# One attention kernel with filling: the maxima of q, k and v and their scales' chains queued behind a tick's row maxima, and the casts and a batch's last splitting spread over more slots

## The chip, the cores and the metric

The kernel runs on one core of a Trainium2 chip. What counts is the device time of one execution in microseconds (us), as a median over several runs. Engines are named as the profile names them: PE is TensorE's matrix multiplication and PEld its loading of weights, DVE is VectorE, ACT is ScalarE, POOL is GpSimd, SP is SyncE, which here issues most of the transfers.

## The reference, cut to what matters

Three stages are chained: block-causal attention, a layer of eight experts with a router, and a gated MLP. Inputs are float32. q and k are drawn with a spread of 0.1 and multiplied by about 3.98.

```python
def _attn_ref(q, k, v):                    # B, H, S, D = 4, 8, 576, 64
    scores = D ** -0.5 * np.matmul(q, k.transpose(0, 1, 3, 2))
    mask = block_i >= block_j              # blocks of 64 positions
    scores = np.where(mask, scores, -1e9)
    attn = np.exp(scores - scores.max(-1))
    attn = attn / (attn.sum(-1) + 1e-9)
    return np.matmul(attn, v)

def _moe_ref(x, w_gate, w1, w2):           # N, D, E, F = 2304, 512, 8, 1024
    P = np.exp(x @ w_gate - (x @ w_gate).max())
    for _ in range(8):
        P /= P.sum(1) + 1e-9
        P /= P.sum(0) + 1e-9
        P *= N / E
    return sum(P[:, e] * (np.maximum(x @ w1[e], 0) @ w2[e]) for e in range(E))

def _moe2_ref(x, w_gate, w_val, w_out):    # 512 -> 1536 -> 512
    g = x @ w_gate
    return (g / (1 + np.exp(-g)) * (x @ w_val)) @ w_out
```

## The kernel before, in words

**The whole.** Matrix products run in float16 with every operand split into a high part and a low part (the cast of a scaled value, and what the cast left out), and 2x2 blocks of matrices are multiplied with seven products instead of eight, over sums and differences of the blocks. So for each operand there is work on ScalarE (the cast, "hi") and on VectorE or POOL (the rest, "lo"). The attention's output goes into `xs`, the seven split operands of the next stage, without a trip to memory. The kernel's rough course is attention with filling to about 350 us, then the experts, then the gated MLP.

**The attention.** `attention` goes over 16 pairs of heads, four to a batch element ("batch" below). A pair takes eight ticks `u` (`TICKS`, L822): u = 0 and 1 hold two score blocks each, u = 2 to 5 one, u = 6 and 7 the two halves of the last. The ticks of the next pair follow without a break, and each tick does a step of several ticks: scores of tick tk (`scores`, L986), their row maxima on VectorE (`maxima`, L999), exponentials of tk - 1 on ScalarE (`exps`, L1016), the reciprocals of the row sums on VectorE (`normalise`, L1031 to L1036) and the scaling on POOL (L1041) of tk - 2, and the transposes on TensorE (L1064, L1073) with the copies on ScalarE (L1067, L1074) of tk - 4. `values` (L1091) multiplies with v at u = 6 and, for the pair before, at u = 4. A tick has three sub-steps, which end in a `yield` each. In each engine the instructions stand in the order in which this code issues them, and an instruction that waits holds up those behind it on its engine. Scores take one of three banks of PSUM (`ps_s`), which a tick frees with its exponentials.

**What lies beside a pair.** From the second batch on, q and k of a pair are split too. `load_qk` loads them, `max_qk` (L917 to L920) takes the maximum of each on VectorE, `across_mid` (L110) brings the maxima of all partitions together with one matmul, `scale_qk` (L116, L156 to L164, L926 to L931) makes the scale from it by a chain of small VectorE operations, `hi_qk` (L937) casts on ScalarE, and `lo_qk` (L941) takes the rest on VectorE and issues the copies into `st` on SP's queue. v needs one scale for a batch: `scan_load`, `scan_max` (L883), `scale_v_begin` (L889), `across_mid`, `scale_v_end` (L895 to L901). `at(tick, f)` (L1164) enters these in a table, and a tick runs its entries first of all, ahead of its scores.

**The output's splitting.** `take` (L1100) writes the attention's output to `xf` (L1106, ScalarE) and puts three or six pieces of splitting work into the queue `pend`: sums on POOL (L1133), casts on ScalarE or POOL (L189, L191), rests on VectorE or POOL (L194, L1124). `work(n)` (L1158) does the first n of them: one or two in a tick, all that is left at u = 4, and at the end of a batch (u = 4 of the next pair) the six new ones at once, after which `ready` says how many rows of the next stage may be worked on.

**Filling.** `first_part` is work of the next stage that runs between the attention's ticks: for the first three of five blocks of 256 rows (`NEARLY` = 3) the router's logits (L1255, L1263) and two expert units (u = 0, 1) with `expert_in` and `plain_out`. While `ready` isn't zero, 47 of 96 sub-steps pull one step of it; what is left after the attention runs by itself. A step of `products_in` (L548) is six matmuls. Sums of products are made on ScalarE (L575) and VectorE (L572, L579, L581, L587), and `plain` turns each of the four sums of a unit into the split operand `m_h`: a cast with Relu on ScalarE (L775) and the rest on VectorE (L779). `later(d, f)` (L510) puts f d slots behind, where a slot is a step of products, that is a call of `tick`. `bank` hands out three banks for these products in turn (their names begin with abc), and `row_bank` gives the small products of `across_mid` one of these as long as `ready` is zero, and one of the scores' banks after that. Through the first half of the attention the weights of both units are split too (`w0`, lines L377, L179, L183).

Names in the profile leave out numbers: `m_h` is the operand of an expert unit, `m_t` and `abc_m_c` a sum and a bank of it, `s` scores, `e` exponentials, `a` the transposed ones, `t` the bank of the transposes, `x` that of the values, `hl` the split q and k, `qk_r`, `qk_e`, `qk_i`, `qk_s` the steps of their scale.

Of the kernel before, what the change touches and what calls it, by code (L numbers as in the profile page):

```python
# [30 lines left out]
def attention_moe_glu_kernel(  # L31
# [724 lines left out]
    def expert_in(u, b, bank):  # L756

        h = hts[u, b] = {}
        if b == BOTH:
            parts = [(units[v][0], *blocks[NB - 1], v == u) for v in (u, u + 1)]  # L760
        else:
            parts = [(units[u][0], *blocks[b], b == NB - 1 or (u % 2 == 1 and u > 1 and b == NB - 2))]
        n = sum(p[2] for p in parts)
        name = f"m{u}_{b}"
        q = {}

        def plain(t, half, src, spare):
            h[t, half] = places.take(f"{name}_h{t}{half}")
            hi, lo = h[t, half][:, 0, :, :n], h[t, half][:, 1, :, :n]
            s = src[:, :, :n]  # L770
            if spare is not None:
                places.give(spare)

            def first():
                nc.scalar.activation(hi, s, AF.Relu)  # L775
                later(1, rest)

            def rest():
                nc.vector.scalar_tensor_tensor(lo, s, 0.0, hi, op0=ALU.max, op1=ALU.subtract)  # L779
                if (t, half) != (1, 0) or b >= NEARLY:  # L780
                    places.give(src)

            if (t, half) == (1, 1):
                later(3 if n == TB else 1, first)
            elif (t, half) == (1, 0) and b >= NEARLY:
                r = places.take(f"{name}_r", F32)
                nc.scalar.copy(r[:, :, :n], s)
                src, s = r, r[:, :, :n]
                later(2, first)
            else:  # L790
                first()

        def quad(t, half, src, spare):
            q[t, half] = src
            if spare is not None:
                q["spare"] = spare
            if (t, half) == (1, 0):
                r = places.take(f"{name}_r", F32)
                nc.scalar.activation(r[:, :, :n], src[:, :, :n], AF.Relu)
                sums_out(h, name, n, q[0, 0], q[0, 1], r, q[1, 1], q["spare"], True)  # L800
                return
            o = {(0, 0): X11, (0, 1): X12, (1, 1): X22}[t, half]
            later(3 if o == X22 and n == TB else 2, lambda: later(1, operand(h, o, name, n, src, AF.Relu)))

        yield from products_in(name, parts, bank, plain if u < 2 else quad)
# [25 lines left out]
    def attention(actx):  # L831
# [19 lines left out]
        zero = const.tile([P, 1], F32, name="zero")  # L851
        nc.gpsimd.memset(zero, 0.0)
        pend = deque()
        for c in range(NC):
            w = ((c + 1) * CB + P - 1) // P * P
            et[c] = ap.tile([P, w], F32, tag=f"e{c}", name=f"e{c}")
            if w > (c + 1) * CB:
                nc.gpsimd.memset(et[c][:, (c + 1) * CB :], 0.0)
# [299 lines left out]
        def work(n):  # L1158
            for _ in range(min(n, len(pend))):
                pend.popleft()()  # L1160

        events = {}

        def at(tick, f, *a):  # L1164
            events.setdefault(tick, []).append(lambda: f(*a))

        for p in range(1, npairs):
            r = p * NTK
            if p < DIRECT:
                if p > 1:  # L1170
                    at(r - NTK, load_direct, p)
                    at(r - 2, lambda p: vt.update({p: load_v(*where(p), "v", 2)}), p)
                continue
            for i in range(2):
                if p > 1:
                    at(r - 14 + 1 * i, load_qk, p, i)
                at(r - 11 + i, max_qk, p, i)
                at(r - 6 + 2 * i, hi_qk, p, i)
                at(r - 5 + 1 * i, lo_qk, p, i)
            at(r - 8, lambda p: across_mid(st[p]["m"]), p)  # L1180
            at(r - 7, scale_qk, p)
            at(r - 2, lambda p: vt.update({p: load_v(*where(p), "v", 2)}), p)
        for b in range(B):
            r = (b - 1) * NPAIR * NTK
            for i in range(NPAIR):
                if b:
                    at(r + i * NTK + (0 if i else 3), scan_load, b, i)
                at(r + i * NTK + NTK if b else 1 + i, scan_max, b, i if b else ORDER[i])
            r = r + NPAIR * NTK if b else NPAIR
            at(r, scale_v_begin, b)  # L1190
            at(r + (2 if b else 1), lambda b: across_mid(vmx[b]), b)
            at(r + (3 if b else 2), scale_v_end, b)

# [12 lines left out]
        for tk in range(tot + NTK):  # L1206
# [7 lines left out]
                scores(p, u)  # L1214
            if u == 6 and p < npairs:
                take(p, 0, values(p, 0))
            yield
            out1 = None
            if on(tk - 4):
                out1 = transposes(*divmod(tk - 4, NTK))  # L1220
            work(2 if len(pend) > 6 else 1)
            if on(tk - 2):
                normalise(*divmod(tk - 2, NTK))
            if out1:
                out1()
            if on(tk):
                maxima(p, u)
            yield

            if p and u == 4:  # L1230
# [1 line left out]
                take(p - 1, 1, values(p - 1, 1))  # L1232
                st.pop(p - 1)
                vt.pop(p - 1)
                if p % NPAIR == 0:
                    work(len(pend))
                    ready[0] = p // NPAIR * S // 2
            if p and u == 3:
                rest(p - 1)()
            if on(tk - 1):  # L1240
                exps(*divmod(tk - 1, NTK))
            yield


# [619 lines left out]
```

## Time and profile before

| what | value |
| --- | --- |
| median of three runs | 2028.02 us (2029.44, 2022.48, 2028.02) |
| the profiled execution | 2023.14 us, its span 2021.4 us |
| TensorE's mean granted clock | 0.99 |
| busy share: PE, DVE, ACT, POOL | 96%, 79%, 68%, 31% |

The span is the time from the first to the last instruction that the profiler recorded in one execution; the profiled execution's own time is 1.7 us longer. "Granted clock" is the share of its full clock (2.4 GHz) that TensorE was given: 0.50 is the lower of its two levels, 1.2 GHz. A mean of 0.99 means that little of the span ran at the lower one. A busy share is an average over stages that are limited by different things, so the rows below come from stretches of the attention and not from the whole.

### The profile page before, as it was taken

Reading aid. Unit: us, or ns where it says so; the run is one execution under the profiler, and the core shown is the slowest. Engines: PE = TensorE matmul, PEld = TensorE weight load, DVE = VectorE, ACT = ScalarE, POOL = GpSimd, SP = SyncE. Lnnn points to the kernel's source line nnn. Section 1 sums busy time; section 2 is a strip of 40 time slices with the busy share of each in tenths; the row PEclk is TensorE's granted clock in tenths of the full one; section 3 lists DMA queues with packets and bytes.
Section 4 is the critical chain, followed back from the end, with each engine's and each line's share of the span. In section 5 each row is a group of like instructions: output and inputs, shape, how many; then the busy total and the mean of one; then the engine's idle time right before and its main releaser. Section 6 shows DMA issues by size and latency. Waiting matters only on the chain. (4 is left out here: it accounts for less than half of the span.)

```text
span 2021.4 us, 47060 instructions
## 1 busy us (share of the span) xinstructions
PE 1939.9 (96%) x18378; PEld 1670.5 (83%) x18378; DVE 1594.6 (79%) x3404; ACT 1382.3 (68%) x2880; POOL 620.5 (31%) x876
## 2 busy tenths in 40 slices
PE   7789999999999999999999999999999889999998
PEld 3457767889888988978888898898889778888987
DVE  8886774888889788798978889778886887667666
ACT  6766775477777788777877877778776656544442
POOL 5544443013333333333333333333332232000000
PEclk9899999999999999999999999999999999999999
DMA  5333432226777786777768768677776100301112
GB/s 154 110 104 112 121 87 63 104 59 136 153 176 158 148 170 129 170 157 160 172 132 167 159 135 178 131 164 162 144 175 152 38 12 17 95 1 53 33 43 53
DMA packets 168079, 236.72 MB, mean 117 GB/s; under 512 B 16432, under 2 KB 84656, under 8 KB 167856
## 3 DMA queue, kind: packets, MB, share of 16 engines
q0 software_dynamic: 67136, 108.29, 31.0%
q1 hardware_dynamic: 100720, 125.42, 19.9%
q8 instruction: 144, 2.36, 0.5%
q14 instruction: 79, 0.65, 0.1%
HBM read 90.39 MB, written 24.38 MB: 57 GB/s over the span
## 5 line engine op out<-in xcount | busy, mean ns | idle before, releaser
L548 PEld LDWEIGHTS <-w 128*128 128x128 f16 x6720 | 609.5, 98 | 79.6 <-issue 16.3
L658 PEld LDWEIGHTS <-m_h 128*128 128x128 f16 x5292 | 513.4, 98 | 69.9 <-issue 6.7
L1519 POOL DMA_DIRECT2D acc<-ev x354 | 311.9, 927 | 576.4 <-ACT ev L1523 377.9
L548 PE MATMUL abc_m_b<-xs,w 128*128 128x256 f16 (+1 forms) x3840 | 474.1, 263 | 7.1 <-ACT m_t L575 3.7
L658 PE MATMUL m_o_b<-w,m_h 128*128 128x256 f16 x3024 | 404.1, 273 | 9.8 <-ACT ev L1523 6.0
L658 PE MATMUL m_o_ac<-w,m_h 128*128 128x256 f16 x2268 | 309.4, 273 | 0.0
L548 PE MATMUL abc_m_c<-xs,w 128*128 128x256 f16 (+1 forms) x1920 | 227.8, 263 | 0.0
L1523 ACT ACTIVATE ev<-m_o_b,pe 128x256 f32<-128x256 f32 x354 | 163.9, 480 | 66.7 <-PE m_o_b L658 45.4
L1523 ACT ACTIVATE ev<-m_o_ac,pe 128x256 f32<-128x256 f32 x236 | 136.3, 580 | 44.5 <-PE m_o_ac L658 43.1
L183 DVE SCALAR_TENSOR_TENSOR w<-wr,ws,w 128x512 f16<-128x512 f32 x210 | 155.6, 750 | 8.3 <-ACT w L179 8.3
L179 ACT ACTIVATE w<-wr,ws 128x512 f16<-128x512 f32 x210 | 150.1, 724 | 17.1 <-DVE ws L164 12.3
L194 DVE TENSOR_TENSOR m_h<-m_t,m_h 128x512 f16<-128x512 f32 x189 | 129.4, 686 | 32.4 <-ACT m_h L696 31.5
L696 ACT CAST m_h<-m_t 128x512 f16<-128x512 f32 x189 | 117.2, 620 | 28.0 <-DVE m_t L720 26.7
L689 ACT ACTIVATE m_h<-m_t 128x512 f16<-128x512 f32 x189 | 118.3, 626 | 23.8 <-DVE m_t L587 14.9
L548 PEld LDWEIGHTS <-gg_w 128*128 128x128 f16 x1260 | 114.6, 98 | 22.0 <-issue 10.0
L693 DVE SCALAR_TENSOR_TENSOR m_h<-m_t,m_h 128x512 f16<-128x512 f32 x189 | 128.5, 684 | 3.1 <-ACT m_h L689 2.8
L1506 POOL DMA_DIRECT2D acc<-ev_s x52 | 63.1, 1213 | 217.0 <-ACT ev_s L1499 211.7
L548 PEld LDWEIGHTS <-gv_w 128*128 128x128 f16 x1260 | 114.5, 98 | 14.0 <-issue 2.2
L658 PEld LDWEIGHTS <-g_h 128*128 128x128 f16 x1134 | 111.5, 99 | 16.3 <-issue 2.3
L1041 POOL TENSOR_SCALAR e<-e,r 128x64 f32<-128x64 f32 (+2 forms) x144 | 84.4, 592 | 124.9 <-DVE r L1036 72.1
L548 PE MATMUL abc_m_a<-xs,w 128*128 128x256 f16 (+1 forms) x960 | 117.5, 262 | 0.0
L572 DVE TENSOR_TENSOR m_t<-m_t,abc_m_b 128x512 f32<-128x512 f32 x73 | 49.4, 677 | 68.2 <-PE abc_m_b L548 60.1
(320 smaller groups left out, 3390.7 us busy)
## 6 DMA issues: line engine op xcount, KB each, us to landing
acc<-ev POOLq DMA_DIRECT2D x354, 256.0 KB, 4.3
wr<-in_w_dram SPq DMA_DIRECT2D x128, 256.0 KB, 5.2
acc<-ev_s POOLq DMA_DIRECT2D x52, 256.0 KB, 3.9
st<-hl SPq DMA_DIRECT2D x48, 144.0 KB, 3.5
raw_g<-in_w_gate_dram SPq DMA_DIRECT2D x12, 512.0 KB, 4.7
raw_v<-in_w_val_dram SPq DMA_DIRECT2D x12, 512.0 KB, 5.2
raw_o<-in_w_out_dram SPq DMA_DIRECT2D x12, 512.0 KB, 5.0
scr_g<-gg SPq DMA_DIRECT2D x21, 256.0 KB, 3.2
```

The source lines that it names most:

```text
L179: nc.scalar.activation(hi, src, AF.Copy, scale=s)
L183: nc.vector.scalar_tensor_tensor(lo, src, s, hi, op0=ALU.mult, op1=ALU.subtract)
L194: nc.vector.tensor_sub(lo, src, hi)
L548: nc.tensor.matmul(ps[:, f, to : to + w], W[o][:, sh, k, f * P : (f + 1) * P], xs[:, o, mh, k, c0 : c0 + w], start=x not in begun, stop=Tr ...
L658: nc.tensor.matmul(ps, h[o][:, sh, k, ii * P : (ii + 1) * P], W[o][:, mh, k], start=o in (X11, X12) and k == 0 and j == 0, stop=True, skip ...
L689: nc.scalar.activation(hi, src, AF.Relu)
L693: nc.vector.scalar_tensor_tensor(lo, src, 0.0, hi, op0=ALU.max, op1=ALU.subtract)
L696: nc.scalar.copy(hi, src)
L1041: nc.gpsimd.tensor_scalar(et[c][:, :n], et[c][:, :n], g["r"][:, c : c + 1], 1.0, op0=ALU.mult, op1=ALU.mult)
L1506: nc.gpsimd.dma_start(acc[:, x - 1 : x + 1, cols], e, accum_op=ALU.add)
L1519: nc.gpsimd.dma_start(acc[:, x], e, accum_op=ALU.add)
L1523: nc.scalar.activation(e[:, cols], ps, AF.Copy, scale=p)
```

## The change

It has three parts. No instruction is added or removed; instructions move in their engines' queues.

1. In `plain`, the rest (L779) of the three early blocks comes two slots behind its cast instead of one, and the cast of a whole block's first two sums joins the queue one slot later instead of at once.
2. At the end of a batch, the six pieces of splitting are no longer done at once: `hurry` counts them, and `hurried()` does one per sub-step, in the other places of a tick too. `ready` is raised when the last is done, six sub-steps later. The last batch still does them at once.
3. `max_qk`, `scale_qk`, `scan_max` and `scale_v_begin` are entered in a second table (`after`, `behind_maxima`), which a tick runs behind its row maxima, at the end of its second sub-step, instead of ahead of its scores. `across_mid`, `scale_v_end`, `hi_qk` and `lo_qk` stay where they were.

```diff
--- before.py
+++ after.py
@@ -773,7 +773,7 @@
 
             def first():
                 nc.scalar.activation(hi, s, AF.Relu)
-                later(1, rest)
+                later(1 if b >= NEARLY else 2, rest)
 
             def rest():
                 nc.vector.scalar_tensor_tensor(lo, s, 0.0, hi, op0=ALU.max, op1=ALU.subtract)
@@ -787,6 +787,8 @@
                 nc.scalar.copy(r[:, :, :n], s)
                 src, s = r, r[:, :, :n]
                 later(2, first)
+            elif n == TB:
+                later(1, first)
             else:
                 first()
 
@@ -851,6 +853,7 @@
         zero = const.tile([P, 1], F32, name="zero")
         nc.gpsimd.memset(zero, 0.0)
         pend = deque()
+        hurry = [0]
         for c in range(NC):
             w = ((c + 1) * CB + P - 1) // P * P
             et[c] = ap.tile([P, w], F32, tag=f"e{c}", name=f"e{c}")
@@ -1159,10 +1162,22 @@
             for _ in range(min(n, len(pend))):
                 pend.popleft()()
 
+        def hurried():
+            if hurry[0]:
+                work(1)
+                hurry[0] -= 1
+                if not hurry[0]:
+                    ready[0] += S // 2
+
         events = {}
 
         def at(tick, f, *a):
             events.setdefault(tick, []).append(lambda: f(*a))
+
+        behind_maxima = {}
+
+        def after(tick, f, *a):
+            behind_maxima.setdefault(tick, []).append(lambda: f(*a))
 
         for p in range(1, npairs):
             r = p * NTK
@@ -1174,20 +1189,20 @@
             for i in range(2):
                 if p > 1:
                     at(r - 14 + 1 * i, load_qk, p, i)
-                at(r - 11 + i, max_qk, p, i)
+                after(r - 11 + i, max_qk, p, i)
                 at(r - 6 + 2 * i, hi_qk, p, i)
                 at(r - 5 + 1 * i, lo_qk, p, i)
             at(r - 8, lambda p: across_mid(st[p]["m"]), p)
-            at(r - 7, scale_qk, p)
+            after(r - 7, scale_qk, p)
             at(r - 2, lambda p: vt.update({p: load_v(*where(p), "v", 2)}), p)
         for b in range(B):
             r = (b - 1) * NPAIR * NTK
             for i in range(NPAIR):
                 if b:
                     at(r + i * NTK + (0 if i else 3), scan_load, b, i)
-                at(r + i * NTK + NTK if b else 1 + i, scan_max, b, i if b else ORDER[i])
+                after(r + i * NTK + NTK if b else 1 + i, scan_max, b, i if b else ORDER[i])
             r = r + NPAIR * NTK if b else NPAIR
-            at(r, scale_v_begin, b)
+            after(r, scale_v_begin, b)
             at(r + (2 if b else 1), lambda b: across_mid(vmx[b]), b)
             at(r + (3 if b else 2), scale_v_end, b)
 
@@ -1214,17 +1229,23 @@
                 scores(p, u)
             if u == 6 and p < npairs:
                 take(p, 0, values(p, 0))
+            hurried()
             yield
             out1 = None
             if on(tk - 4):
                 out1 = transposes(*divmod(tk - 4, NTK))
-            work(2 if len(pend) > 6 else 1)
+            if hurry[0]:
+                hurried()
+            else:
+                work(2 if len(pend) > 6 else 1)
             if on(tk - 2):
                 normalise(*divmod(tk - 2, NTK))
             if out1:
                 out1()
             if on(tk):
                 maxima(p, u)
+            for f in behind_maxima.pop(tk, ()):
+                f()
             yield
 
             if p and u == 4:
@@ -1232,13 +1253,17 @@
                 take(p - 1, 1, values(p - 1, 1))
                 st.pop(p - 1)
                 vt.pop(p - 1)
-                if p % NPAIR == 0:
+                if p == npairs:
                     work(len(pend))
-                    ready[0] = p // NPAIR * S // 2
+                    ready[0] = B * S // 2
+                elif p % NPAIR == 0:
+                    hurry[0] = len(pend)
             if p and u == 3:
                 rest(p - 1)()
             if on(tk - 1):
                 exps(*divmod(tk - 1, NTK))
+            if u != 4:
+                hurried()
             yield
 
 
```

What moves is seen in the order of the instructions on an engine. The first place is VectorE at the start of pair 7, while block 0's first unit is worked on. In the rows, `vmx` is the maximum of v, `bias` that of the rows, and `qk_r` to `sc` the chain of the next pair's q and k. Before:

```order
L779 SCALAR_TENSOR_TENSOR m_0_h_1882<-m_0_t_1880,m_0_h_1882 128x512
L883 TENSOR_REDUCE vmx_1286<-vs_2_1619 128x1
L999 ISA junk,bias_1971<-qk_a,zero,sc_1671 128x64
L999 ISA bias_1971 128x1
L999 ISA junk,bias_1971<-qk_a,zero,sc_1671 128x128
L999 ISA bias_1971 128x1
L779 SCALAR_TENSOR_TENSOR m_0_h_1998<-abc_m_0_b,m_0_h_1998 128x512
L116 TENSOR_REDUCE qk_r<-qk_a 128x2
L156 TENSOR_SCALAR qk_e<-qk_r 128x2
L163 TENSOR_SCALAR qk_i<-qk_e 128x2
L164 RECIPROCAL qk_s<-qk_i 128x2
L931 TENSOR_SCALAR sc_2011<-qk_i 128x1 x2
```

With the change (the lines are three further down in the file):

```order
L779 SCALAR_TENSOR_TENSOR m_0_h_1882<-m_0_t_1880,m_0_h_1882 128x512
L1002 ISA junk,bias_1946<-qk_a,zero,sc_1676 128x64
L1002 ISA bias_1946 128x1
L1002 ISA junk,bias_1946<-qk_a,zero,sc_1676 128x128
L1002 ISA bias_1946 128x1
L886 TENSOR_REDUCE vmx_1294<-vs_2_1594 128x1
L587 TENSOR_TENSOR m_0_t_1823<-m_0_t_1823,abc_m_0_c 128x512
L1034 TENSOR_SCALAR r_1600<-sum_1599 128x1
L1039 RECIPROCAL r_1600<-r_1600 128x1
L1002 ISA junk,bias_1946<-s_1_1976,zero,sc_1676 128x192
L1002 ISA bias_1946 128x1
L1002 ISA junk,bias_1946<-s_1_1976,zero,sc_1676 128x256
```

The maximum of v now stands behind the first row maxima, and the chain of q and k has left these rows: it follows the row maxima of u = 1, whose last is the row 128x256.

The second place is ScalarE at the end of pair 6 and the start of pair 7, with two casts of `plain` to `m_h` and the copies of the transposed exponentials to `a`. Before:

```order
L1016 ACTIVATE e_140,sum_1624<-s_5_1844,bias_1623,sc_1338 128x512
L775 ACTIVATE m_0_h_1942<-m_0_t_1742 128x512
L775 ACTIVATE m_0_h_1882<-m_0_t_1880 128x512
L1074 COPY a_6_1904<-t_3_1946 128x3x128
L1074 COPY a_6_1904<-t_4_1982 128x4x128
L775 ACTIVATE m_0_h_1998<-abc_m_0_b 128x512
L1016 ACTIVATE e_141,sum_1624<-s_6_1891,bias_1623,sc_1338 128x288
L1016 ACTIVATE e_141,sum_1624<-s_7_1930,bias_1623,sc_1338 128x288
L1074 COPY a_6_1904<-t_5_2036 128x4x128
```

With the change:

```order
L1019 ACTIVATE e_140,sum_1599<-s_5_1825,bias_1598,sc_1341 128x512
L1077 COPY a_6_1884<-t_3_1919 128x3x128
L1077 COPY a_6_1884<-t_4_1957 128x4x128
L1019 ACTIVATE e_141,sum_1599<-s_6_1861,bias_1598,sc_1341 128x288
L1019 ACTIVATE e_141,sum_1599<-s_7_1908,bias_1598,sc_1341 128x288
L775 ACTIVATE m_0_h_1938<-m_0_t_1936 128x512
L775 ACTIVATE m_0_h_1992<-m_0_t_1823 128x512
L1077 COPY a_6_1884<-t_5_1995 128x4x128
```

The two casts have moved from ahead of two copies and two exponentials to behind them; the next copy still follows them.

The third place is ScalarE at the end of the first batch, u = 4 to 6 of pair 4. `xs` are the casts of the batch's last splitting, `w` is weights' splitting. Before:

```order
L1106 ACTIVATE xf_3_1_1120<-x_1_1109,vs_263 128x320
L191 CAST xs<-xf_3_1_1120 128x160 x2
L191 CAST xs<-xf_2_1_863 128x160
L1016 ACTIVATE e_137,sum_948<-s_3_1064,bias_947,sc_742 128x384
L1067 COPY a_4_1099<-t_1_1152 128x2x256
L179 ACTIVATE w_1_0_1162<-wr_0_00_884,ws_0_1138 128x512
L1263 COPY lsb_1197<-abc_lg_1164 128x64
L1016 ACTIVATE e_138,sum_948<-s_4_1094,bias_947,sc_742 128x448
```

With the change:

```order
L1109 ACTIVATE xf_3_1_1120<-x_1_1109,vs_263 128x320
L1019 ACTIVATE e_137,sum_943<-s_3_1064,bias_942,sc_759 128x384
L191 CAST xs<-xf_3_1_1120 128x160 x2
L1070 COPY a_4_1099<-t_1_1139 128x2x256
L179 ACTIVATE w_1_0_1154<-wr_0_00_884,ws_0_1125 128x512
L1019 ACTIVATE e_138,sum_943<-s_4_1094,bias_942,sc_759 128x448
L191 CAST xs<-xf_2_1_863 128x160
```

The three casts no longer stand together ahead of the exponential of u = 3, and the logits' copy `lsb` has left these rows, since filling starts later.

## Rows read from the trace of the kernel before

**Rows 1.** Busy time by window: us, busy (instructions), PEclk, DMA share, GB/s.

```profile
58.00:92.00 34.00, 27.50 (x201) 15.30 (x202) 29.13 (x104) 22.95 (x62) 21.51 (x46) 0.80 0.52 145
92.00:142.00 50.00, 39.54 (x355) 27.35 (x354) 45.34 (x140) 37.16 (x94) 20.68 (x41) 0.98 0.36 105
169.00:346.00 177.00, 171.94 (x1618) 125.89 (x1617) 121.53 (x444) 121.84 (x328) 81.35 (x185) 1.00 0.31 88
```

The busy columns are PE, PEld, DVE, ACT and POOL, in this order.

**Rows 2.** The same view, the windows of lower clock.

```profile
75.20:82.00 6.80, 6.07 (x23) 2.96 (x25) 6.10 (x25) 3.65 (x10) 4.57 (x14) 0.50 0.31 84
85.40:88.80 3.40, 3.40 (x48) 2.52 (x46) 2.65 (x13) 1.72 (x4) 2.24 (x6) 0.50 0.84 218
140.04:146.87 6.83, 5.33 (x29) 3.64 (x30) 5.94 (x22) 3.69 (x9) 2.12 (x5) 0.50 0.16 47
```

**Rows 3.** Timeline: start, duration, engine, line, [idle before, its releaser].

```profile
139.11 0.67 DVE L587 TENSOR_TENSOR m_t<-m_t,abc_m_c 128x512 f32<-128x512 f32 x1
139.88 1.15 ACT L775 ACTIVATE m_h<-m_t 128x512 f16<-128x512 f32 x2 [2.88 <-DVE m_t L587]
...
141.54 1.09 PE L1073 MATMUL t<-ident,e 128*128 128x128 f32 x4 [3.54 <-ACT a L1074]
```

**Rows 4.** Timeline, TensorE: waits behind ScalarE at four other places.

```profile
104.62 0.41 PE L1064 MATMUL t<-ident,e 128*128 128x128 f32 x2 [1.26 <-ACT a L1074]
...
113.81 0.44 PE L986 MATMUL s<-st,st 128*64 128x288 f16 x4 [1.26 <-ACT xf L1106]
...
228.44 0.63 PE L1073 MATMUL t<-ident,e 128*128 128x128 f32 x4 [0.80 <-ACT a L1074]
...
312.73 0.63 PE L1073 MATMUL t<-ident,e 128*128 128x128 f32 x4 [1.14 <-ACT a L1074]
```

**Rows 5.** Timeline, the end of the first batch's splitting.

```profile
84.12 0.33 ACT L191 CAST xs<-xf 128x160 f16<-128x160 f32 x1 [0.23 <-POOL xf L1133]
...
85.16 0.84 PE L986 MATMUL s<-st,st 128*64 128x512 f16 x4 [2.01 <-ACT e L1016]
```

**Rows 6.** Timeline, three pairs' starts, and a step of filling.

```profile
75.60 1.11 PE L1073 MATMUL t<-ident,e 128*128 128x128 f32 x4 [2.32 <-POOL e L1041]
...
76.02 0.55 ACT L1016 ACTIVATE e<-s,bias,sc 128x256 f32<-128x256 f32 x1
...
76.86 0.96 PE L986 MATMUL s<-st,st 128*64 128x448 f16 x4
...
90.31 0.82 PE L548 MATMUL abc_m_b<-xs,w 128*128 128x256 f16 x6
...
100.68 0.66 PE L1073 MATMUL t<-ident,e 128*128 128x128 f32 x4 [1.31 <-POOL e L1041]
...
120.28 0.41 DVE L116 TENSOR_REDUCE qk_r<-qk_a 128x2 f32<-128x256 f32 x1
...
121.14 0.17 DVE L164 RECIPROCAL qk_s<-qk_i 128x2 f32<-128x2 f32 x1
...
121.56 0.77 ACT L937 ACTIVATE hl<-qk,qk_s 128x576 f16<-128x576 f32 x1
...
124.05 0.51 ACT L1016 ACTIVATE e<-s,bias,sc 128x192 f32<-128x192 f32 x1 [1.72 <-DVE bias L999]
...
124.14 0.66 PE L1073 MATMUL t<-ident,e 128*128 128x128 f32 x4 [1.90 <-POOL e L1041]
```

**Rows 7.** Timeline, two splittings of VectorE and POOL's scaling.

```profile
140.54 0.69 DVE L779 SCALAR_TENSOR_TENSOR m_h<-m_t,m_h 128x512 f16<-128x512 f32 x1 [0.76 <-ACT m_h L775]
...
141.90 0.69 POOL L1041 TENSOR_SCALAR e<-e,r 128x512 f32<-128x512 f32 x1 [2.52 <-DVE r L1036]
...
142.13 1.00 DVE L779 SCALAR_TENSOR_TENSOR m_h<-m_t,m_h 128x512 f16<-128x512 f32 x1
```

**Rows 8.** Timeline, TensorE at the end of the attention.

```profile
346.11 2.27 PE L1091 MATMUL x<-a,v 128*64 128x320 f32 x20 [0.73 <-ACT a L1074]
...
349.01 0.55 PE L1255 MATMUL m_lg<-wg,xs 128*128 128x16 f16 x15 [0.62 <-ACT xf L1106]
```

## The prediction

> **What bounds the kernel now.** I read the page's busy shares first, then the views in this order: busy time by stretch, the stretches at half clock, the timeline at each of TensorE's longer waits, and the order of instructions of both kernels. Over the whole span TensorE is busy 96%, so time can be gained only where it idles or runs at half clock. The instruction orders of both kernels are the same from the third block's logits on, but for two casts and their splittings in one block; whatever happens, happens in the first 370 us. [Rows 1] split the attention by stretch. From 169 to 346 us TensorE is busy 171.9 of 177 us: filling has closed its gaps, and a shorter wait elsewhere gives nothing. From 58 to 142 us it is different: TensorE idles 6.5 of 34 and 10.5 of 50 us, while VectorE is busy 29.1 of 34 and 45.3 of 50. There a tick's chain (scores, row maxima on VectorE, exponentials on ScalarE, reciprocals on VectorE, scaling on POOL, transposes on TensorE, copies on ScalarE) runs beside the weights' splitting for both experts, and VectorE and the queue orders set the pace. [Rows 2] are the three stretches in which the granted clock fell to 0.50, each around a place where TensorE had waited; at half clock a stretch costs half its length where TensorE has work, so 3.4, 1.7 and 3.4 us.
>
> **The casts of filling.** In [rows 3] ScalarE stands 2.88 us before two casts to m_h, because they wait for VectorE's add L587, which had to queue (it starts at 139.11). Behind the casts stands the copy a<-t, and TensorE's next transposes wait 3.54 us for it; the clock then stays at 0.50 until 146.87 [rows 2]. The same chain (cast waits for an add, a copy or an xf behind it, TensorE behind that) is at 104.62, 113.81, 228.44 and 312.73 us [rows 4]: 1.26, 1.26, 0.80 and 1.14 us. The change lets the cast join ScalarE's queue a slot later and its splitting two slots later; no instruction is added. In the new order the casts of this place stand behind two copies and two exponentials. At 141.54 the upper bound is 3.54 + 3.4 = 6.9 us. I take 4.5, because the second cast still needs L587, which now stands behind the row maxima, vmx and a splitting, so part of the wait stays, with the next copy behind it. Of 0.80 + 1.14 = 1.9 us in the later batches I take 1.5. The two of 1.26 go into the sum for 58 to 142 us below.
>
> **The batch's last splitting.** At 84.12 ScalarE does the third of three xs casts ahead of the exponential of tick u=3, after waiting for POOL; TensorE's scores of u=5 wait 2.01 us for that exponential [rows 5], and 85.4 to 88.8 us run at half clock. In the new order the exponential comes first. Six pieces of POOL, ScalarE and VectorE work are the same in number. The broadcast w_a also goes to another bank, since `ready` is still zero, so the scores of u=5 no longer need the bank of u=3. Upper bound: 2.0 + 1.7 = 3.7 us here; at the two later batch ends only waits under half a microsecond stand.
>
> What this costs: filling starts six sub-steps (two ticks) later in each batch. It has 292 sub-steps instead of 298, at 47 steps in 96, that is 142 steps where three blocks need 135 and some waiting, so it still ends inside the attention. But about three steps leave the stretch that VectorE paces, where they were hidden, for the one that TensorE paces: 3 x 0.82 us (six matmuls of L548) [rows 6] = 2.5 us at most, 0 at least. I take 1.5. At the far end the same three steps then stand between the last values and the logits, where TensorE waits 0.73 and 0.62 us today [rows 8]: I take a gain of 1.0 of 1.35.
>
> **The maxima and chains.** The q and k chain takes VectorE from 120.28 to 121.31 [rows 6], 1.03 us, and two small operations follow. It stands ahead of the reciprocals of the pair before, whose scaling on POOL TensorE's transposes wait for: 1.90 us at 124.14, and in the same place 2.32 at 75.60 and 1.31 at 100.68 [rows 6]. Queued behind the row maxima, the chain no longer delays them: at most 3 x 1.03 = 3.1 us. But at 124.14 two m_h splittings now stand in the old place of the chain (2 x 0.69 us), so that one keeps its wait.
>
> The new wait: the hi cast of q (L937) precedes the exponentials of u=1 in ScalarE's queue in both orders. Before, the cast started at 121.56 and the exponential waited for its bias until 124.05 [rows 6]. Now the bias is ready 1.03 us sooner, but the cast waits for a chain that starts only then: 1.03 + 0.77 us after the bias, so the exponential comes 0.77 us later than before. Behind it are the scores of u=4, which need that bank. The bound from below is 0 (in the TensorE-paced batches there are some 5 us between u=1 and u=4), from above 0.77 for each of 12 pairs, 9.2 us. I take about three pairs of the VectorE-paced stretch, 2.0 us.
>
> A splitting that meets POOL runs longer: at 142.13 it takes 1.00 us beside POOL's scaling at 141.90, against 0.69 at 140.54 [rows 7]. Of block 0's eight splittings, all would cost 8 x 0.31 = 2.5 us of VectorE if each newly met one; they meet some today, so I put nothing in the sum and keep this for the range. The Trainium skill (GPSIMD Engine Reference, Key points) says that POOL shares its SBUF interfaces with VectorE and contends with VectorE instructions of two SBUF inputs; the trace agrees with the 1.00 against 0.69.
>
> **The sum.** From 58 to 142 us the separate waits that can go are 1.26 + 1.26 + 2.01 + 1.7 + about 2.1 (75.60 and 100.68) = 8.3 us. VectorE does the same work, and idles 4.9 + 4.7 = 9.5 us there [rows 1], part of it in the tiny gaps between dependent instructions; so I take about half, 4.5. Then: -4.5 (58 to 142) - 4.5 (141.54 and its clock) - 1.5 (later batches) - 1.0 (tail) + 2.0 (hi cast) + 1.5 (filling's steps) = **-8.0 us**. The profiled execution took 2023.14 us (span 2021.4), 4.9 below the median of the three runs, 2028.02; the forecast is 2015.1 on its scale, and 2020.0 on the median's.
>
> **Rivals.**
> A: VectorE is the bound from 58 to 142 us, and the waits only change places. For it: the shares of [rows 1]; no VectorE work is removed, and splittings move into the places that the chains leave. Against: VectorE itself idles in places that the change touches, as behind the burst. Then the 4.5 there is 0, a new wait of the casts keeps half of the 4.5 at 141.54, and -2.2 - 1.5 - 1.0 + 2.0 + 1.5 leaves about -1 to -2: 2026. The Trainium skill (Perfetto Trace Analysis, Identifying the Most-Contended Engine) says to optimise the engine with the highest occupancy first; by that rule this stretch would give nothing, and the trace agrees that VectorE's is the highest there (45.34 of 50 us against TensorE's 39.54).
> B: slower. The hi cast makes ScalarE late in every pair: 12 x 0.77 = 9.2 us, filling's steps cost their full 2.5, and of the gains only the 4.5 at 141.54 stays: +7.2, 2035. It decides from the point at which the exponentials of u=1 end after TensorE has reached the scores of u=4. For it: the first time, u=4's scores start at 76.86, 0.29 us behind the end of u=1's second exponential (76.02 + 0.55) [rows 6]. Against: [rows 1], TensorE paces eight of the twelve pairs and hides this.
> C: everything goes through, 8.3 + 6.9 + 1.9 + 1.35 = 18.5 us less, no cost: 2009.5. For it: the waits are caused by queue order alone. Against: VectorE's shares.
> That the change doesn't do what it says is excluded by the orders.
>
> **Chances.** Forecast (2 to 14 us less) 0.60, A 0.18, B 0.13, C 0.09. A difference of 0.3%, 6 us, is about what a measurement can tell (the three runs lie 7 us apart). Of the forecast's 0.60, 0.44 is over 6 us and 0.16 under; A gives 0.16 no change and 0.02 slower; so faster 0.53, same 0.32, slower 0.15. Range 2007 to 2031: from C and a little scatter below it, up to the lower part of B; the forecast's own is 2014 to 2026.
>
> **What would show it.** Right: in the profile after, no wait of TensorE over 2 us on a<-t around 140 us and no half clock there; the scores of u=5 in pair 4 within 1 us of the values; the attention's last values product at about 338 instead of 346 us; the same stage lengths after that. The chain: POOL's scaling for the last transposes of a pair starts about 1 us sooner against the scores of u=2, and ScalarE waits for qk_s ahead of the hi cast. Wrong: new half-clock stretches between 86 and 110 us, where filling is now missing; VectorE over 93% busy from 58 to 142 us with the stretch no shorter (A); ScalarE's waits before the hi cast adding up to over 5 us (B); or a difference that arises after 370 us, for which I have no mechanism.

## The result, and the profile after

The changed kernel is slower: 2041.03 us median (four runs, 2040.34 to 2043.92) against 2028.65 (2022.48 to 2029.44), a ratio of 1.007 with a 95% interval of 1.0054 to 1.0086. The forecast was 2020.0, faster, and the range ended at 2031. The profiled execution took 2041.31 us, 18.2 more than the one before, while the medians differ by 12.4: the profiled execution before (2023.14 us) was one of its kernel's quicker ones, so a difference of a few us between two profiles can be scatter.

The tops of the two pages show the same number of instructions on each engine in a longer span. Before:

```profile
PE 1939.9 (96%) x18378; PEld 1670.5 (83%) x18378; DVE 1594.6 (79%) x3404; ACT 1382.3 (68%) x2880; POOL 620.5 (31%) x876
```

Changed:

```profile
span 2039.5 us, 47054 instructions
...
PE 1943.4 (95%) x18378; PEld 1669.8 (82%) x18378; DVE 1595.1 (78%) x3404; ACT 1383.2 (68%) x2880; POOL 621.0 (30%) x876
```

**Where the time went.** The table gives the length of each batch's stretch, from the first scores of pairs 0, 4, 8 and 12 and to the last scores of pair 15 (first matmul of L986 and L975, or their later line numbers). Behind them, the stretch to a wait that both kernels have, TensorE's for the sum `m_t` in block 3 (365.13 us before, 380.97 after), takes 31.2 and 31.5 us. What follows that wait differs by 2.3 us between the two profiled executions (1656.2 and 1658.5).

| kernel | pairs 0 to 3 | 4 to 7 | 8 to 11 | 12 to 15 |
| --- | --- | --- | --- | --- |
| before | 62.9 | 100.6 | 84.4 | 80.4 |
| changed | 68.5 | 99.5 | 91.3 | 84.8 |

The loss is where I had expected least: 5.6 us in the first batch, 6.9 and 4.3 in the two that TensorE paces. The busy time by window, with the boundaries of the last three stretches (columns as in [rows 1]), before:

```profile
68.49:169.08 100.59, 83.89 (x720) 58.01 (x719) 81.74 (x272) 66.35 (x172) 46.08 (x97) 0.92 0.37 109
169.08:253.48 84.40, 82.35 (x777) 59.60 (x776) 63.69 (x230) 59.52 (x160) 40.53 (x94) 1.00 0.39 112
253.48:333.92 80.44, 78.06 (x742) 56.27 (x741) 54.02 (x202) 56.86 (x154) 37.60 (x84) 1.00 0.26 73
```

Changed:

```profile
73.94:173.42 99.48, 80.87 (x685) 53.98 (x684) 79.30 (x265) 65.31 (x169) 44.71 (x95) 0.93 0.36 104
173.42:264.69 91.27, 85.29 (x776) 60.68 (x776) 63.76 (x231) 60.29 (x160) 41.16 (x94) 0.98 0.36 104
264.69:349.44 84.75, 80.64 (x740) 57.27 (x740) 54.53 (x207) 56.65 (x152) 38.80 (x85) 0.98 0.25 70
```

TensorE has got idle time in the last two, 6.0 and 4.1 us instead of 2.1 and 2.4, and the clock's mean is 0.98 where it was 1.00. Over the whole execution the mean granted clock is no lower, 0.991 against 0.99, so stretches of half clock have changed their places and are not more. What TensorE waited for up to 363 us, before and then with the change (releaser, us in total, times, longest), is the next view. Before:

```profile
PE t L1073 <- POOL e L1041: 8.8, 7, 2.3
PE t L1073 <- ACT a L1074: 6.1, 6, 3.5
PE s L986 <- ACT e L1016: 3.3, 2, 2.0
```

Changed:

```profile
PE s L989 <- ACT e L1019: 14.2, 11, 4.4
PE t L1076 <- POOL e L1044: 4.8, 5, 1.7
PE t L1076 <- ACT a L1077: 3.4, 6, 0.8
PE qk_a L110 <- DVE r L1038: 3.4, 4, 1.0
PE abc_v L110 <- DVE r L1038: 3.2, 1, 3.2
...
PE qk_a L110 <- DVE qk_d L103: 1.3, 3, 0.7
```

The waits that the change was to shorten did get shorter (8.8 to 4.8 and 6.1 to 3.4 us). Two others came: scores wait for exponentials, 14.2 us, and the small matmuls of the maxima (L110) wait for VectorE.

**The first new wait.** The timeline of the changed kernel at the start of pair 5:

```profile
104.21 0.42 DVE L116 TENSOR_REDUCE qk_r<-qk_a 128x2 f32<-128x256 f32 x1
...
104.66 0.41 ACT L1019 ACTIVATE e<-qk_a,bias,sc 128x64 f32<-128x64 f32 x1 [4.23 <-DVE qk_r L116]
...
105.65 0.85 PE L989 MATMUL s<-st,st 128*64 128x384 f16 x4 [4.36 <-ACT e L1019]
...
106.11 0.76 ACT L940 ACTIVATE hl<-qk,qk_s 128x576 f16<-128x576 f32 x1
```

`qk_a` is one bank of PSUM with two things in it: the scores of u = 0 and, in its last 256 columns, the maxima of the next pair's q and k (`row_bank`). The chain's first reduction reads the one, the exponential the other; the program orders them, the exponential waits 4.23 us for a reduction that it needs nothing from, and the scores of u = 3, which need that bank, wait 4.36. It is not the cast of q, as the prediction had it: here that starts behind the exponential without a wait. The predicted wait does come in pairs 3 and 4, where `ready` is still zero and the maxima have a bank of their own: the cast of q waits 1.61 and 2.77 us for the chain (at 60.18 and 81.14), and the scores of u = 4 wait 2.07 and 1.96 us for the exponential behind it (at 62.81 and 83.00). Before, they waited 1.43 us and not at all. The kernel before already has the order on the shared bank, at a small price:

```profile
120.73 0.40 ACT L1016 ACTIVATE e<-qk_a,bias,sc 128x64 f32<-128x64 f32 x1 [0.17 <-DVE qk_r L116]
```

The Trainium skill (PSUM — Partial Sum Buffer, PSUM bank collisions raise a hardware error) says that two engines must not be in the same partitions of one bank at once, two readers included; the order that the trace shows agrees with that, and no run here shows what would happen without it.

**The second new wait.** The end of pair 8 and the start of pair 9, TensorE and VectorE, before:

```profile
187.28 0.74 DVE L920 TENSOR_REDUCE qm<-qk 128x1 f32<-128x576 f32 x1
...
187.94 0.51 DVE L103 TENSOR_SCALAR qk_d<-ident,qm 128x128 f32<-128x128 f32 x2
...
189.74 0.60 PE L110 MATMUL qk_a<-qk_d,ones 128*128 128x256 f32 x2
```

Changed:

```profile
192.76 0.73 DVE L1002 CUSTOM_DVE_ANT_0 junk<-s,zero,sc 128x512 bf16<-128x512 f32 x1
...
193.42 0.75 DVE L923 TENSOR_REDUCE qm<-qk 128x1 f32<-128x576 f32 x1
...
194.81 0.50 DVE L1002 CUSTOM_DVE_ANT_0 junk<-s,zero,sc 128x288 bf16<-128x288 f32 x1
...
195.24 0.75 DVE L923 TENSOR_REDUCE qm<-qk 128x1 f32<-128x576 f32 x1
...
195.90 0.82 DVE L103 TENSOR_SCALAR qk_d<-ident,qm 128x128 f32<-128x128 f32 x2
...
196.77 1.04 PE L110 MATMUL qk_a<-qk_d,ones 128*128 128x256 f32 x2 [1.02 <-DVE r L1038]
```

Before, `qk_d`, from which TensorE brings the maxima together, was ready at 188.45, and L110 took it at 189.74: 1.29 us of slack. Now the second maximum (195.24) follows the row maxima of u = 6, and `qk_d` is ready at 196.72, 1.02 us late. TensorE's instruction stayed where it was, ahead of the scores of the new pair, and all of TensorE stands behind it. It is the same in the other pairs: before, L110 started 0.24 to 3.84 us behind its `qk_d`, and in the changed kernel it starts within 0.1 us of it in nine of the twelve. From 197.00 to 200.41 us the granted clock is 0.50. The same kind of wait, for v in pair 0, was 1.50 us before:

```profile
13.00 0.49 PE L110 MATMUL abc_v<-v_d,ones 128*128 128x128 f32 x2 [1.50 <-DVE r L1035]
```

In the changed kernel it is 3.24:

```profile
13.00 0.81 DVE L886 TENSOR_REDUCE vmx<-v_first 128x1 f32<-128x640 f32 x1
...
14.38 0.49 PE L110 MATMUL abc_v<-v_d,ones 128*128 128x128 f32 x2 [3.24 <-DVE r L1038]
```

### The profile page after: what moved, and what is told of

Read it like the earlier page. It is cut to its first block, busy times and chain, and to the rows that moved or that the text cites. A ratio compares the mean times of both kernels' runs of the same rounds, so it can differ in the third digit from the quotient of the medians.

```text
span 2039.5 us, 47054 instructions
## 1 busy us (share of the span) xinstructions
PE 1943.4 (95%) x18378; PEld 1669.8 (82%) x18378; DVE 1595.1 (78%) x3404; ACT 1383.2 (68%) x2880; POOL 621.0 (30%) x876
## 3 DMA queue, kind: packets, MB, share of 16 engines
q8 instruction: 144, 2.36, 0.5%
## 5 line engine op out<-in xcount | busy, mean ns | idle before, releaser
L548 PEld LDWEIGHTS <-w 128*128 128x128 f16 x6720 | 609.6, 98 | 81.0 <-issue 17.3
L548 PE MATMUL abc_m_b<-xs,w 128*128 128x256 f16 (+1 forms) x3840 | 475.2, 263 | 7.7 <-ACT m_t L575 4.0
L548 PE MATMUL abc_m_c<-xs,w 128*128 128x256 f16 (+1 forms) x1920 | 227.8, 263 | 0.0
L548 PEld LDWEIGHTS <-gg_w 128*128 128x128 f16 x1260 | 113.8, 98 | 21.8 <-issue 10.3
L548 PEld LDWEIGHTS <-gv_w 128*128 128x128 f16 x1260 | 114.4, 98 | 16.0 <-issue 3.8
L548 PE MATMUL abc_m_a<-xs,w 128*128 128x256 f16 (+1 forms) x960 | 118.6, 263 | 0.0
```

Of the source, the lines that this page charges most:

```text
L548: nc.tensor.matmul(ps[:, f, to : to + w], W[o][:, sh, k, f * P : (f + 1) * P], xs[:, o, mh, k, c0 : c0 + w], start=x not in begun, stop=Tr ...
```

## The experiments

Medians of before in these comparisons were 2026.7 to 2027.6 us. Rows have the line numbers of the changed kernel, except those of the run that only releases filling later, which has the numbers of the kernel before.

**Each group of moves alone.** The third part alone on the kernel before, with the first two undone:

> The kernel before with the third part of the change alone (maxima of q, k, v and the chains behind the row maxima). Theory W (the third part makes two new waits): the reduction of the q and k chain reads the PSUM bank that holds the scores of u = 0, so that tick's exponential waits for it and the scores of u = 3 wait for the exponential (4.36, 3.61, 1.50, 0.81 and 1.01 us in the changed kernel); and the small matmuls of the maxima wait for VectorE (3.24 us at 14 us, seven of 0.67 to 1.02 us later). By it this kernel is as slow as the change or slower, 2039 to 2050 us, with waits of over 1 us at u = 3 of pairs 5 and 6. Theory F (the shifted filling of the first two parts costs the time in the batches that TensorE paces): 2026 to 2033 us.

Measured: 2036.68 us, ratio 1.0043 (1.0031 to 1.0056). Slower, so the third part carries most of the loss (10.0 us against 12.4 for the whole change, each against its own before); it is below the range expected. The changed kernel without the third part (four `after(...)` back to `at(...)`):

```diff
-                after(r - 11 + i, max_qk, p, i)
+                at(r - 11 + i, max_qk, p, i)
-            after(r - 7, scale_qk, p)
+            at(r - 7, scale_qk, p)
-                after(..., scan_max, b, i if b else ORDER[i])
+                at(..., scan_max, b, i if b else ORDER[i])
-            after(r, scale_v_begin, b)
+            at(r, scale_v_begin, b)
```

> The changed kernel with the third part undone: casts and a batch's last splitting spread, maxima and chains where they were. Theory W: faster than before, 2012 to 2023 us, with no wait over 1 us at u = 3 and none over 0.7 us at the small matmuls behind the first 20 us. Theory F: 2034 to 2042 us, and pairs 8 to 10 and 12 to 14 as long as in the changed kernel (24.3, 21.3, 21.2, 24.0, 21.0, 19.7 us).

Measured: 2027.43 us, 1.0002 (0.9993 to 1.0011). Neither theory: the loss is gone, but nothing is gained, so the first two parts give nothing together. The pairs 8 to 11 take 87.4 us, 3.0 more than before, and a wait of over 1 us at u = 3 is still there (1.59 us at 238.26). The q and k chain alone put back (only `scale_qk` to `at`):

> The changed kernel with the q and k chain alone put back ahead of a tick's scores; the maxima of q, k and v and the start of v's scale stay behind the row maxima. Theory W: the waits at u = 3 go (11.3 us and some half clock), the waits at the small matmuls stay (some 7 us and half clock at 16, 197 and 289 us): 2025 to 2033 us. If the shared bank were not the cause of the waits at u = 3: they stay, 2037 to 2042 us.

Measured: 2039.29 us, 1.0057 (1.0044 to 1.0071). And the counterpart, the chain alone behind (the other three back to `at`):

> The changed kernel with the maxima of q, k and v and the start of v's scale put back, and the q and k chain alone behind the row maxima. Theory W: the waits at u = 3 stay, those at the small matmuls go: 2028 to 2036 us, and the wait at 14 us is about 1.5 us again instead of 3.24. If the late maxima were the main cause: 2015 to 2024 us.

Measured: 2027.39 us, 1.0002 (0.9993 to 1.0011). Both lie outside the ranges of theory W, and they decide it: the chain's move costs nothing net (2027.39 with it, 2027.43 without), and the maxima's moves cost all. In the run before that one the waits of scores for exponentials had indeed gone down, from 14.2 to 6.7 us, and those of transposes for POOL up, from 4.8 to 9.4. My theory that the longer of the new waits is the dearer one falls. What TensorE waits for says why. Without the chain's move (run e2_no_chains):

```profile
PE t L1076 <- POOL e L1044: 9.5, 7, 2.3
PE s L989 <- ACT e L1019: 7.9, 7, 2.6
```

With it (run e4_only_chain):

```profile
PE s L989 <- ACT e L1019: 16.8, 16, 4.3
...
PE t L1076 <- POOL e L1044: 3.5, 3, 1.7
```

The chain delays the reciprocals in one place and the exponentials in the other: +8.9 us of the one wait against -6.0 of the other, and TensorE is as late either way.

**Which maxima, and why.** With v's put back (`scan_max` and `scale_v_begin` to `at`), and then with q's and k's a tick earlier as well:

> The changed kernel with v's maxima and the start of its scale put back; the maxima of q and k and the chain stay behind the row maxima. All the maxima behind cost some 13 us (2041 against 2027 us with the chain alone behind). Theory Q (q and k's share is most: TensorE's small matmul at the start of a pair comes 1 us late in each, and the clock falls after some): 2034 to 2039 us, with the first pair's length back at 12.8 to 14.3 us. Theory V (v's share is most): 2027 to 2031 us.

Measured: 2035.79 us, 1.0049 (1.0036 to 1.0061). So q and k's share is most, as theory Q has it. The loss is 9.1 us against this run's own before (2026.73), where the whole change lost 12.4 against its own (2028.65); that leaves 3.3 us for v, or 5.2 if the two medians are compared as they are (2041.03 - 2035.79). The first batch is back from 68.5 to 64.7 us.

```diff
-                after(r - 11 + i, max_qk, p, i)
+                after(r - 12 + i, max_qk, p, i)
```

> As the run with v's maxima put back, but with the maxima of q and k entered one tick earlier, still behind a tick's row maxima. If the cost is that they come too late for the small matmul of TensorE at the pair's start, it goes: 2024 to 2030 us, and no wait over 0.5 us at that matmul. If the cost is that VectorE's queue holds them at all behind the row maxima (what stands behind them is late instead), it stays: 2034 to 2039 us.

Measured: 2026.83 us, 1.0002 (0.9991 to 1.0013). One tick earlier, with the same instructions still behind the row maxima, gives the whole 9.0 us back. The waits of the run before this one

```profile
PE qk_a L110 <- DVE r L1038: 3.4, 4, 1.0
...
PE qk_a L110 <- DVE qk_d L103: 1.3, 3, 0.7
```

are not in the list of the run with the earlier maxima. So it is not that VectorE holds the maxima behind row maxima; it is that TensorE's matmul that takes them up stayed at its tick. These waits add up to 4.7 us; the rest of the 9.0 isn't split further here. The counterpart, the maxima at their late place and L110 a tick later, was not run.

**Casts and splitting apart.** The first part alone on the kernel before, and the second alone:

> The kernel before with the first part alone: filling's casts and their splittings join the queues later. The first two parts together gave nothing (2027.43 against 2026.71 us). Theory C (the casts' waits go, as the prediction has it, and the second part's later filling gives it back): 2019 to 2024 us, and the wait of 3.54 us at 141.54 is gone. Theory M (a cast that waits for its sum holds up whatever stands behind it on ScalarE, so the wait moves to the next thing in the queue): 2025 to 2029 us, with new waits of over 0.7 us on an exponential or a copy.

Measured: 2024.91 us, 0.999 (0.998 to 1.0001): some 2 us faster, just not told from none. The wait at the end of pair 6 is still there (3.10 us at 142.76), though theory C had it gone.

> The kernel before with the second part alone: a batch's last splitting spread over six sub-steps, filling six sub-steps later. Theory C: 2028 to 2034 us, slower than before, since filling's steps move to where TensorE sets the pace. Theory M: 2024 to 2029 us: the wait of 2.01 us at the first batch's end gets smaller, and the shifted filling's casts meet other places of the ticks, for better or worse.

Measured: 2033.33 us, 1.0034 (1.0021 to 1.0046), slower, as theory C has it. Then the shift of filling without the spread splitting:

```diff
                     work(len(pend))
-                    ready[0] = p // NPAIR * S // 2
+                    late[0] = tk + 2
...
+            if late[0] and (late[0] == tk or p == npairs):
+                ready[0] += S // 2
+                late[0] = 0
```

> The kernel before with filling released two ticks later in each batch, as the second part does, but a batch's last splitting still done at once. The second part alone was slower (2033.3 us). Theory S (its cost is the shift of filling: its casts meet other places of the ticks, and the exponential of u = 0 stands behind them): 2030 to 2037 us, with waits of over 1.5 us at u = 3 of the last pairs of batches, as there. Rival (the spread splitting itself holds up the queues): 2024 to 2028 us.

Measured: 2034.93 us, 1.004 (1.0025 to 1.0054). Releasing filling two ticks later costs 7 us by itself, with all else as before. Its timeline at the start of pair 11:

```profile
237.36 0.42 DVE L116 TENSOR_REDUCE qk_r<-qk_a 128x2 f32<-128x256 f32 x1
...
238.84 0.68 DVE L587 TENSOR_TENSOR m_t<-m_t,abc_m_c 128x512 f32<-128x512 f32 x1
...
239.55 1.15 ACT L775 ACTIVATE m_h<-m_t 128x512 f16<-128x512 f32 x2 [2.23 <-DVE m_t L587]
...
241.07 0.41 ACT L1016 ACTIVATE e<-qk_a,bias,sc 128x64 f32<-128x64 f32 x1
...
242.06 0.52 PE L986 MATMUL s<-st,st 128*64 128x384 f16 x4 [2.36 <-ACT e L1016]
```

The casts of a unit's last sums, which met a pair's last copies before ([rows 3, 4]), now meet the exponential of u = 0 of the next pair, whose bank TensorE needs; and the sum they wait for stands behind the chain on VectorE. In [rows 4] that wait was 0.80 us, here it is 2.36. With the spread casts of the first part it is 1.59 us (at 238.26 in the run without the third part), and all waits of scores (L986 or its later number) for exponentials add up to 7.9 us there and to 12.4 with the second part alone. That goes with the first two parts together losing 0.7 us where the second alone loses 6.6; how the spread casts do it is not shown further.

**The chain behind the exponentials.** `scale_qk` is issued behind the exponentials of u = 0, all maxima where they were; VectorE's order is that of the run with the chain alone behind (cut to the new place):

```diff
             if on(tk - 1):
                 exps(*divmod(tk - 1, NTK))
+            if tk in behind_exps:
+                f, x = behind_exps.pop(tk)
+                f(x)
```

> The changed kernel with all maxima put back, and the q and k chain issued behind the exponentials of u = 0 instead of ahead of them; VectorE's order is that of the run with the chain alone behind (2027.4 us). There the exponential of u = 0 waits for the chain's first reduction, which reads the bank of its scores, and TensorE waits 16.8 us in all at scores for exponentials. Theory B (that order on the shared bank makes these waits): they fall to 4 to 8 us, the waits of transposes for POOL stay at about 3.5 us, 2018 to 2023 us. Rival H (the cast of q, late behind its chain, makes the next exponential late instead): the waits move to the scores of u = 4, 2025 to 2031 us.

Measured: 2030.35 us, 1.0016 (1.0005 to 1.0026), within rival H's range and some 3 us slower than the run that it was to improve. TensorE, then ScalarE:

```profile
PE s L989 <- ACT e L1019: 9.5, 9, 2.0
PE s L989 <- DVE qk_r L116: 8.9, 4, 3.3
```

```profile
ACT hl L940 <- DVE qk_s L164: 17.9, 11, 3.7
```

The exponential no longer waits, but the bank is free only when both have read it: the scores of u = 3 now wait for the reduction itself, 8.9 us. So the bank is held by whichever reader is last, and neither order of the two frees it sooner while the chain stands late on VectorE. And ScalarE waits 17.9 us before the cast of q, in 11 pairs, with waits of 1.0 to 2.0 us at the scores of u = 4 in six of them: that is the prediction's rival B as it was described.

> The kernel before with the first part (casts spread, 2024.9 us alone) and the q and k chain issued behind the exponentials of u = 0; no second part, maxima where they were. Theory B: 2016 to 2021 us. Rival H: 2023 to 2029 us.

Measured: 2031.63 us, 1.002 (1.0009 to 1.0031), above both ranges. Each against its own before, it loses 4.1 us where the casts alone gain 1.8: the chain behind the exponentials costs some 6 us without the second part too.

**A version made from these.** The maxima are put back as in the first diff above; the rest of the edit:

```diff
-            after(r - 7, scale_qk, p)
+            (after if p <= 2 * NPAIR else at)(r - 7, scale_qk, p)
...
+                if p == NPAIR:
+                    hurry[0] = len(pend)
                 elif p % NPAIR == 0:
-                    hurry[0] = len(pend)
+                    work(len(pend))
+                    ready[0] = p // NPAIR * S // 2
```

> A version made from what the runs showed: the first part as it is; the second part at the end of the first batch alone, so that filling of the later blocks isn't shifted again; the q and k chain behind the row maxima only for the pairs whose chain runs before pair 8, where VectorE sets the pace; all maxima where they were before. If the stretches add up, pairs 4 to 7 take 96 to 98 us (100.6 before), pairs 8 to 11 84 to 86 us (84.4 before; 87.4 with chain and shift), pairs 12 to 15 79.9 to 80.5 us as with the casts alone, together 2020 to 2025 us. If each shift of the filling only moves the waits, 2025 to 2030 us.

Measured: 2027.07 us, 1.000 (0.9991 to 1.001). Pairs 4 to 7 take 97.0 us, as hoped, but pairs 8 to 11 take 87.8 and the last batch 81.8. What pairs 4 to 7 gain is mostly work put off: their stretch holds 264 of filling's matmuls (L548, L614) instead of 300, and the next two hold 384 and 348 instead of 360 and 336. 36 matmuls are 4.9 us by [rows 6] (0.82 us for six), and pairs 4 to 7 gained 3.6. No version that was run beats the kernel before by more than its interval.

## Why the prediction was wrong

- **The step that failed** is in the part on the maxima and chains. It priced the chain that moves (`scale_qk`), on VectorE and on ScalarE, and gave the move of `max_qk`, `scan_max` and `scale_v_begin` no term at all. Their consumer is an instruction of TensorE with a fixed place (`across_mid`, not moved): a tick's delay of the producer became a wait of the engine that sets the pace. The missing term measured +9.0 us for q and k and +3.3 to +5.2 for v, together the whole loss of 12.4. The danger could have been read from the kernel before: the slack between `qk_d` and L110 was as short as 0.24 us, and the move used it up in most pairs. The prediction also took the batches that TensorE paces as safe from new waits; in the profiles they are 6.9 and 4.3 us longer.
- **The new wait: +2.0 us for the cast of q.** The wait came as described in pairs 3 and 4 alone, where it cost TensorE 0.6 and 2.0 us more than before. In the later pairs the new wait behind the chain is another one: the bank that chain and scores share; the prediction had looked at a shared bank only at the splitting's place, and the 0.17 us at 120.73 before showed this one. Net of the waits for POOL that went, the chain's move measured 0 (2027.39 against 2027.43), where the prediction had it gain up to 3.1 and lose 2.0.
- **-4.5 us for the wait at 141.54.** That wait went: in the changed kernel nothing over 0.8 us stands on a copy to `a`, and pair 7 takes 25.0 us instead of 31.4. But the casts alone leave it (3.10 us, pair 7 31.4 us). It gets smaller when filling is shifted, since the casts then fall elsewhere, and the time comes back there: with the shift alone pair 7 takes 27.9 us, and pair 6 takes 30.8 instead of 21.8.
- **-1.5 us for the later batches** had, if any, the right sign for the casts alone, with which pairs 8 to 11 and 12 to 15 are 0.3 and 0.5 us shorter. With the shift of filling it is the wrong one: pairs 8 to 11 take 3.0 us more with the first two parts alone, since the shifted casts meet the exponential of u = 0.
- **+1.5 us for filling's steps and -1.0 at the tail.** The three steps hold twelve matmuls each, not six: pairs 4 to 7 hold 264 of filling's matmuls instead of 300, 4.9 us where 2.5 was the upper bound. But they did not go to the batches that TensorE paces, which hold 360 and 336 as before. They went behind pair 15: the stretch there has 297 matmuls instead of 261 and is only 0.3 us longer (31.5 against 31.2), for the waits of [rows 8] are gone, and its mean granted clock is 1.00 where it was 0.95. The larger error was to price only the number of steps and not their place: the shift alone costs 7 us.
- **-4.5 us from 58 to 142 us**: pairs 4 to 7 became 1.1 us shorter with 4.9 us less of filling in them, and TensorE's idle time in them went from 16.7 to 18.6 us, so the waits in it only changed places, as rival A has it. The term's wait of 2.01 us at the batch's last splitting did go (the scores of u = 5 follow the values at 88.87), but 84.36 to 87.77 still run at half clock. A's reason is not borne out: VectorE's busy share fell, from 81.3% (81.74 of 100.59 us) to 79.7% (79.30 of 99.48), which speaks against the amount of its work as the bound.
- **The rivals.** B had the sign and was nearest in time (2035), for a reason that decides little here. Of what should show the forecast right, the wait at 140 us and its half clock did go, the scores of u = 5 in pair 4 did start within 1 us of the values, and the stages behind were nearly as long as before; the attention's last values product came at 363.45, 17 us later and not 8 sooner. Of what should show it wrong, a new half clock between 86 and 110 us came (104.84 to 111.66), behind the wait of 4.36 us for the shared bank and not for lack of filling.

## What to carry to other kernels

When an instruction is queued later on one engine, look up who takes its result and whether that consumer has moved too: a producer moved without its consumer costs nothing while the delay is smaller than the slack between the two, and TensorE's time when it is larger, as here, where the slack was 0.24 to 3.84 us. If both a critical and a small side result live in one bank or buffer, moving the side result's reader moves the release of the bank. And the start of background work is a phase, not only an amount: two ticks' shift put the same instructions behind other waits and cost as much as the tuned waits were worth.

## What the runs showed of the hardware that was not expected

The clock doesn't fall at every wait of the same length. In the changed kernel the wait of 1.02 us at 196.77 is followed by 3.4 us at 0.50:

```profile
197.00:200.41 3.41, 3.41 (x21) 2.22 (x21) 2.47 (x9) 0.00 (x0) 1.46 (x6) 0.50 0.15 41
```

In the run with v's maxima put back, the same wait at the same place (1.02 us at 193.63) is followed by a granted clock of 1.00, and ahead of both TensorE did the same instructions. So a stretch of half clock behind one wait is a poor measure of what that wait costs; what decides between the two stays open.
